# Rows gathered for the experts: transposed by TensorE instead of by DMA, and an expert's weight preparation moved into the next expert's first tile

## The chip, the core and the metric

The kernel runs on one core of a Trainium2 chip. The metric is the device time in microseconds (us) of one execution. Three runs of the kernel before took 850.43, 850.56 and 857.25 us; the median is 850.56.

## The reference: what is computed

Three layers follow each other. An attention over chunks of 64 positions (4 batches, 8 heads, 576 positions of 64) gives 2304 rows of 512 values. A mixture of 8 experts sends each row to the one expert with the largest gate value, and a plain two-matrix network with a hidden width of 2048 ends it (called FFN below).

```
x = attention(q, k, v)                       # 2304 rows of 512
probs = softmax(x @ w_gate); e = argmax      # one expert for each row
for each row i that expert e keeps:
    h = max(x[i] @ w1[e], 0)                 # 512 -> 1024
    out[i] = gate[i] * (h @ w2[e])           # 1024 -> 512
h = out @ w_in;  g = h * sigmoid(h);  result = g @ w_out      # FFN
```

## The kernel before, in words

Attention comes first and stores each row of x in the DRAM tensor `x_d`, as 512 high and 512 low halves in 16 bits and a factor. The experts follow, from 150.8 to 437.0 us of the profiled execution, then the FFN up to the end.

**A tile** (`moe_tile`, line 832) is up to 128 rows of one expert. Here the experts have 4, 1, 4, 3, 2, 1, 3 and 2 tiles, 20 in all, called t1 to t20 below (expert 0 has t1 to t4, expert 1 has t5, expert 2 t6 to t9, expert 3 t10 to t12, expert 4 t13 and t14, expert 5 t15, expert 6 t16 to t18, expert 7 t19 and t20). On TensorE (PE) a tile is 2 halves of 48 matmuls into `mh` (line 845), each value a sum of three products of high and low halves, and then 8 groups f = 0 to 7 of 3 matmuls into `myp` (line 866). Behind each half, ScalarE (ACT) writes `hh` (line 850) and VectorE (DVE) `hl` (line 851). The groups f = 0 to 3 read `hh` and `hl` of the first half, f = 4 to 7 those of the second. At the end the rows are scaled and scattered to `y_d` by a transfer that GpSimd (POOL) issues (line 882).

**A tile's rows** come by an indirect transfer on POOL (`gather`, line 819) into `xg`. The SyncE queue (SP) then issues a transfer that transposes them into `mxT` (`t_dma`, line 830, 128x8x128 values of 16 bits). SP runs its issues in the order of the program, and its transposes stand between the loads of weights (`w_piece`, lines 134 and 136) and of FFN weights (`f_load`, line 779).

**An expert's weights** (`w_prep`, lines 145 to 179) are two matrices, m = 0 (w1) and m = 1 (w2), of four 512 KB pieces each. Each piece is loaded, squared and summed on ACT (`sq`, line 157); the four sums are added over the partitions by a matmul with ones on PE (`red`, line 124, into the bank `fh`); DVE makes a scale of them (`sc`, lines 163 and 102 to 104); POOL writes the scaled high halves (`hi`, line 172) and DVE the low halves (`lo`, line 175). The buffer of a piece is loaded again once its low half is done (`lo_ld`, line 990).

**What sets the order.** The program is written out expert by expert. The first tile of an expert (j = 0) always runs; the code of the others stands in a branch on the count of rows (`more`, line 930), with an Else that does the rest of the preparation if the tile doesn't run. Work for the next expert is put into five places of the first tile (`slots`, 997 to 1004: 0 at its start, 1 behind the first half, 2 and 3 behind the second half, 4 at f = 6) and of the second and third tile (`arms`, 1035 to 1037). Before the change, `sq`, `red` and `sc` of the first matrix of the expert after next stand in the arms, `red` at f = 6 of the second tile or in the Else; `hi` of that matrix stands in slot 0 of the next expert's first tile, so it starts without a wait for a sum. The FFN weights are converted to 16 bits in the arms too (`f_conv`, lines 794 to 802), with the sums of squares of `w_in` on ACT (line 808).

The lines that the steps of the prediction touch: 819, 830, 845, 851, 866, 882 (tile), 124, 157, 163, 172, 175 (weights), 930 (branches), 439 and 444 (the transposes that the attention part already does on PE, with the copy out of PSUM on ACT).

Of the kernel before, what the change touches and what calls it, by code (L numbers as in the profile page):

```python
# [22 lines left out]
def attention_moe_ffn_kernel(  # L23
# [748 lines left out]

    def f_load(k):
# [54 lines left out]
    def t_dma(e, j):  # L828
        xg = xg_s[2 * (e % 2) + j % 2]
        nc.sync.dma_start_transpose(out=xT_s[slot(e, j)], in_=xg.bitcast(F16)[:, 0:2 * DM])  # L830

    def moe_tile(e, j, tok_i, c_i, keep, nxt, bg):
# [27 lines left out]
        for f in range(KF1):  # L860
            if f == 3 * KF1 // 4:
                bg(4)
                nxt(1)
# [29 lines left out]
    def t_next(e, j):  # L893
        t_dma(e, j)
        t_f1(e, j)
# [21 lines left out]
    t_dma(0, 1)  # L917
# [11 lines left out]
    def more(e, j, arms):  # L929
        with tc.If(n_e[e] > P * j) as cmp:  # L930
            def nxt(k):
                if k < 0 and j + 1 < NJ:
                    t_dma(e, j + 1)
                if k == 0 and j + 1 < NJ:
                    t_f1(e, j + 1)
                if k == 0 and j + 2 < NJ:
                    g_next(e, j + 2)
# [42 lines left out]
    m_dg = [st_s[1][3][:, (t + 1) * P:(t + 2) * P] for t in range(4)]  # L980
    for e in range(E):
# [4 lines left out]
        if not last:  # L986
            _, _, _, hi1, lo1 = prep[e + 1, 0]
# [9 lines left out]
            slots[0] = [lambda: g_next(e + 1, 0), *[lambda c=c: hi1(c) for c in range(4)]] if e else []  # L997
            slots[1] = [l1s[0], lambda: sq2(0), lambda: sq2(1)]
            slots[2] = [lambda: sq2(2), lambda: sq2(3), l1s[1], l1s[2], l1s[3]]
            slots[3] = [*([g2] if e else []), lambda: g_next(e + 1, 1)]  # L1000
            slots[4] = [red2, sc2, *[lambda c=c: hi2(c) for c in range(4)]]
        else:
            sp = [lambda c=c: f_split(0, c) for c in range(NSP)]
            slots = [[*cb, *cn], [], [], [], [lambda: f_red(0), lambda: f_sc(0), *sp]]

        def nxt0(k):
            if k < 0:
                if 0 < e < E - 1:
                    t_dma(e, 1)
            elif k == 0:  # L1010
                t_f1(e, 1)
                if last:
                    g_next(e, 2)
                else:
                    t_dma(e + 1, 0)
# [12 lines left out]
        if not last:  # L1028
            sqs, red, sc = [], [], []
            if e + 2 < E:  # L1030
                sq, r, c1, _, _ = prep[e + 2, 0]
                sqs, red, sc = [lambda c=c: sq(c) for c in range(4)], [r], [c1]
            arms[0] = [*l2s, *sqs, *red, *cb, *cn, *sc]
            arms[1] = [l2s[0:1], [l2s[1], *sqs[0:2]], [*l2s[2:4], *sqs[2:4], cb[0], cn[0]], [], [*red, *sc]]
            arms[2] = [[], cb[1:2], [*cb[2:], *cn[1:]], [], []]
        else:
            arms[0] = []
        more(e, 1, arms)
        if e + 2 == E:
            t_dma(E - 1, 1)  # L1040
# [214 lines left out]
```

## Time and profile before

| | |
|---|---|
| median of three runs | 850.56 us |
| the profiled execution: its time, and the span that the profile shows | 850.38 us, 848.6 us |
| PE busy | 722.5 us, 85% of the span |
| VectorE, POOL, ACT busy | 448.1, 359.4, 333.2 us |
| start of t1, of the FFN | 150.76, 437.02 us |

PE is the busiest engine, so the question for each piece of work is whether PE waits for it. A row of the timeline is a start, a duration, the engine, the line, the operation with the tile that it writes and those it reads, a count, and in brackets how long the engine was idle before it and what ended that. Consecutive equal instructions stand in one row.

### The profile page before, as it was taken

What the parts mean: (1) busy time and instruction counts of PE and PEld (TensorE: products, weight loads), DVE (VectorE), ACT (ScalarE), POOL (GpSimd) and SP (SyncE); (2) the same over time, 40 slices, a digit from 0 to 9 for tenths busy, and PEclk for the clock granted to TensorE, in tenths of its full rate; (3) what the DMA queues carried; (4) which work ended last, traced back from release to release, by engine and by line L of the source; (5) the groups of instructions that cost most, each with busy time, mean ns of one, the idle gap of its engine ahead of it and who ended that gap; (6) DMA issues with size and microseconds to landing.
All of it is one profiled execution on the core that took longest, in us unless ns stands there. A gap on an engine that the chain in (4) does not pass through costs nothing.

```text
span 848.6 us, 14692 instructions
## 1 busy us (share of the span) xinstructions
PE 722.5 (85%) x5526; PEld 440.5 (52%) x5526; DVE 448.1 (53%) x920; ACT 333.2 (39%) x615; POOL 359.4 (42%) x355
## 2 busy tenths in 40 slices
PE   4798764998489989569798776999999999999995
PEld 3677654765456756447553333444444444565442
DVE  4365886654794758678339999633322223222000
ACT  5586737443443536442134455322232223223010
POOL 3475632524571737665167535544223223212111
PEclk9797955899699999979899999999999999999999
DMA  7988983992986798895635235020001000001000
GB/s 170 230 231 206 191 239 59 306 273 56 303 246 162 177 235 239 241 237 123 135 72 102 73 125 124 1 51 1 1 37 38 1 1 37 14 1 39 13 37 38
DMA packets 133325, 103.20 MB, mean 122 GB/s; under 512 B 85472, under 2 KB 112096, under 8 KB 133216
## 3 DMA queue, kind: packets, MB, share of 16 engines
q1 hardware_dynamic: 126784, 83.41, 40.2%
q0 software_dynamic: 5760, 18.39, 7.3%
q8 instruction: 60, 0.98, 0.5%
q14 instruction: 49, 0.40, 0.2%
q10 hardware_dynamic: 672, 0.02, 0.0%
HBM read 73.45 MB, written 14.71 MB: 104 GB/s over the span
## 4 chain that ended last, share of the span: by engine, by line
PE 30%; DVE 8%; issue 7%; DMA 4%; POOL 2%; ACT 1%; POOLq 0%; ACTq 0%; DVEq 0%
PE ops L1143 14%; PE fh L1115 14%; DMA out_dram<-ob,yrow 3%; DVE g L1126 2%; DVE th L1121 2%; DVE wot L797 1%; DVE wot L802 1%; PE mh L845 1%; DVE wot L794 1%; DVE win L734 1%; DMA y_d<-yr,tabs 1%; PE myp L866 0%; POOL win L751 0%; POOL win L749 0%; POOL win L750 0%
## 5 line engine op out<-in xcount | busy, mean ns | idle before, releaser
L1143 PE MATMUL ops<-wot,gh 128*128 128x512 f16 x576 | 171.3, 379 | 0.0
L1115 PE MATMUL fh<-yT,win 128*128 128x512 f16 (+1 forms) x768 | 156.9, 355 | 7.0 <-DVE g L1126 7.0
L1130 POOL TENSOR_TENSOR gl<-g,gh 128x512 f16<-128x512 f32 (+1 forms) x80 | 91.9, 1151 | 163.8 <-ACT gh L1128 163.8
L1115 PEld LDWEIGHTS <-win 128*128 128x128 f16 x960 | 94.2, 98 | 118.1 <-issue 26.1
L845 PE MATMUL mh<-mxT,wsp 128*128 128x128 f16 x1920 | 125.6, 233 | 17.7 <-PEq L930 9.4
L845 PEld LDWEIGHTS <-wsp 128*128 128x128 f16 x1920 | 123.5, 106 | 24.1 <-issue 19.9
L1143 PE MATMUL ops<-wot,gl 128*128 128x512 f16 x288 | 109.2, 379 | 0.0
L1121 DVE TENSOR_TENSOR th<-fh,rb 128x512 f32<-128x512 f32 (+1 forms) x64 | 39.8, 622 | 130.7 <-PE fh L1115 130.7
L1122 ACT ACTIVATE th<-th,fi 128x512 f32<-128x512 f32 (+1 forms) x80 | 54.3, 679 | 133.8 <-DVE th L1121 132.9
L175 DVE SCALAR_TENSOR_TENSOR wsp<-st,s,wsp 128x1024 f16<-128x1024 f32 x64 | 99.6, 1591 | 6.0 <-POOL wsp L172 6.0
L866 PE MATMUL myp<-wsp,hh 128*128 128x512 f16 x320 | 96.5, 384 | 0.0
L1143 PEld LDWEIGHTS <-gh 128*128 128x128 f16 x576 | 56.4, 98 | 64.1
L172 POOL TENSOR_SCALAR wsp<-st,s 128x1024 f16<-128x1024 f32 x56 | 75.2, 1359 | 20.0 <-DVE inv L104 11.4
L1128 ACT CAST gh<-g 128x512 f16<-128x512 f32 (+1 forms) x80 | 45.9, 574 | 73.2 <-DVE g L1126 54.3
L157 ACT ACTIVATE junk<-st 128x1024 bf16<-128x1024 f32 x64 | 67.4, 1053 | 16.4 <-DMA st<-in_moe_w_dram 15.3
L1126 DVE TENSOR_TENSOR g<-fh,th 128x512 f32<-128x512 f32 (+1 forms) x80 | 50.7, 634 | 38.8 <-ACT th L1122 32.4
L866 PE MATMUL myp<-wsp,hl 128*128 128x512 f16 x160 | 61.6, 385 | 8.2 <-DVE hl L851 8.0
L819 POOL DMA_INDIRECT xg<-x_d,tabs x34 | 45.4, 1336 | 35.2 <-issue 9.5
L882 POOL DMA_INDIRECT y_d<-yr,tabs x20 | 23.5, 1175 | 79.3 <-DVE yr L879 36.8
L851 DVE SCALAR_TENSOR_TENSOR hl<-mh,hh 128x512 f16<-128x512 f32 x40 | 27.5, 687 | 48.3 <-ACT hh L850 48.3
L1115 PE MATMUL fh<-st,win 128*128 128x512 f16 x192 | 43.5, 379 | 10.6 <-DVE g L1126 9.3
L866 PEld LDWEIGHTS <-hh 128*128 128x128 f16 x320 | 30.7, 101 | 29.8 <-ACT hh L850 0.8
(194 smaller groups left out, 849.8 us busy)
## 6 DMA issues: line engine op xcount, KB each, us to landing
st<-in_moe_w_dram SPq DMA_DIRECT2D x64, 512.0 KB, 6.4
fs<-in_moe_w_in_dram SPq DMA_DIRECT2D x16, 512.0 KB, 7.0
fs<-in_moe_w_out_dram SPq DMA_DIRECT2D x16, 512.0 KB, 3.4
vbd<-in_v_dram SPq DMA_DIRECT2D x72, 64.0 KB, 3.4
x_d<-xr SPq DMA_DIRECT2D x9, 512.0 KB, 6.1
ku<-in_k_dram SPq DMA_DIRECT2D x6, 512.0 KB, 5.7
qu<-in_q_dram SPq DMA_DIRECT2D x6, 512.0 KB, 8.3
ku<-in_k_dram SPq DMA_DIRECT2D x2, 384.0 KB, 4.2
```

Of the source, the lines that this page charges most:

```text
L157: nc.scalar.activation(out=junk, in_=st[c], func=ACTF.Square, accum_out=n2[:, c:c + 1])
L172: hi_eng.tensor_scalar(sp[c][:, 0, :], st[c], s, 1.0, ALU.mult, ALU.mult)
L175: lo_eng.scalar_tensor_tensor(out=sp[c][:, 1, :], in0=st[c], scalar=s, in1=sp[c][:, 0, :], op0=ALU.mult, op1=ALU.subtract)
L845: nc.tensor.matmul(out=ps[:, f4, :], lhsT=a[c][:, part, f0:f0 + P], rhs=xt[:, rc, :], start=(n == 0), stop=(n == 3 * KD - 1),)
L866: nc.tensor.matmul(out=yp, lhsT=lh[:, f % 4, :], rhs=b[f // 2][:, part, (f % 2) * DM:(f % 2 + 1) * DM], start=(n == 0), stop=(n == 3 * KF1 ...
L1115: nc.tensor.matmul(out=hp[:, 0:n], lhsT=wv[:, part, c, :], rhs=yT_t[b](rc, n), start=(i == 0), stop=(i == 3 * KD - 1),)
L1121: nc.vector.tensor_tensor(out=th[:, 0:n], in0=hp[:, 0:n], in1=rb_t[b][:, 0:n], op=ALU.mult)
L1122: nc.scalar.activation(out=th[:, 0:n], in_=th[:, 0:n], func=ACTF.Sigmoid, scale=fi[:, 0:1])
L1126: nc.vector.tensor_tensor(out=g[:, 0:n], in0=hp[:, 0:n], in1=th[:, 0:n], op=ALU.mult)
L1128: nc.scalar.copy(out=gh[:, 0:n], in_=g[:, 0:n])
L1130: nc.gpsimd.tensor_tensor(out=gl[:, 0:n], in0=g[:, 0:n], in1=gh[:, 0:n], op=ALU.subtract)
L1143: nc.tensor.matmul(out=o_t[b][t], lhsT=lh[:, t * P:(t + 1) * P], rhs=wv[:, part, :], start=(f == 0 and i == 0), stop=(f == KFF - 1 and i = ...
```

## The change

The transposing transfer is removed. `x_tr` puts 8 PE transposes of 128x128 into one PSUM bank (the second of the two `fh` banks) and copies the bank to `mxT` on ACT. It is called behind the second half of each tile for the tile after it, and at f = 4 of an expert's first tile for the next expert's first tile. `red`, `sc` and `hi` of an expert's first matrix move to slot 1 of the expert before it, between the two halves of its first tile. The sums of squares of `w_in` (`cn`) move from the arms to slot 2 of the next expert.

```diff
--- before.py
+++ after.py
@@ -770,6 +770,8 @@
     ps_s = [mps.tile([P, 4, P], F32, name=f"mh{i}") for i in range(4)]
     yp_s = [mps.tile([P, DM], F32, name=f"myp{i}") for i in range(2)]
 
+    xtp = fh_s[1].bitcast(F16).rearrange("p (c t) -> p c t", c=2 * KD)
+
     def f_load(k):
         if k >= 2 * KFF:
             return
@@ -825,9 +827,11 @@
         f1 = f1_s[slot(e, j)]
         nc.vector.tensor_scalar(f1, xg[:, DM:DM + 1], w_fac[e, 0], w_fac[e, 1], ALU.mult, ALU.mult)
 
-    def t_dma(e, j):
-        xg = xg_s[2 * (e % 2) + j % 2]
-        nc.sync.dma_start_transpose(out=xT_s[slot(e, j)], in_=xg.bitcast(F16)[:, 0:2 * DM])
+    def x_tr(e, j):
+        xh = xg_s[2 * (e % 2) + j % 2].bitcast(F16)
+        for c in range(2 * KD):
+            nc.tensor.transpose(out=xtp[:, c, :], in_=xh[:, c * P:(c + 1) * P], identity=ident16)
+        nc.scalar.copy(out=xT_s[slot(e, j)], in_=xtp)
 
     def moe_tile(e, j, tok_i, c_i, keep, nxt, bg):
         xt, f1 = xT_s[slot(e, j)], f1_s[slot(e, j)]
@@ -858,6 +862,8 @@
         yp = yp_s[1 if j else 0]
         n = 0
         for f in range(KF1):
+            if f == KF1 // 2:
+                nxt(2)
             if f == 3 * KF1 // 4:
                 bg(4)
                 nxt(1)
@@ -891,7 +897,7 @@
         gather(e, j, tabs[:, 0, e, j:j + 1])
 
     def t_next(e, j):
-        t_dma(e, j)
+        x_tr(e, j)
         t_f1(e, j)
 
     def rest(e):
@@ -914,7 +920,6 @@
     t_next(0, 0)
     g_next(0, 1)
     g_next(1, 0)
-    t_dma(0, 1)
     w_load(1, 1)
     p10[1]()
     g_next(0, 2)
@@ -929,9 +934,8 @@
     def more(e, j, arms):
         with tc.If(n_e[e] > P * j) as cmp:
             def nxt(k):
-                if k < 0 and j + 1 < NJ:
-                    t_dma(e, j + 1)
                 if k == 0 and j + 1 < NJ:
+                    x_tr(e, j + 1)
                     t_f1(e, j + 1)
                 if k == 0 and j + 2 < NJ:
                     g_next(e, j + 2)
@@ -978,13 +982,14 @@
     NSP = 4
     conv_of = [[2 * e, 2 * e + 1] for e in range(E - 2)] + [[2 * E - 4, 2 * E - 3, 2 * E - 2], [2 * E - 1]]
     m_dg = [st_s[1][3][:, (t + 1) * P:(t + 2) * P] for t in range(4)]
+    cn_prev = []
     for e in range(E):
         last = e + 1 == E
         ops = [f_conv(c) for c in conv_of[e]]
         cb, cn = [lambda o=o: [f() for f in o[0:3]] for o in ops], [o[3] for o in ops]
         slots = [[], [], [], [], []]
         if not last:
-            _, _, _, hi1, lo1 = prep[e + 1, 0]
+            _, red1, sc1, hi1, lo1 = prep[e + 1, 0]
             sq2, red2, sc2, hi2, lo2 = prep[e + 1, 1]
 
             def lo_ld(m, c):
@@ -994,25 +999,27 @@
 
             l1s, l2s = [[lambda m=m, c=c: lo_ld(m, c) for c in range(4)] for m in range(2)]
             g2 = lambda: g_next(e, 2)
-            slots[0] = [lambda: g_next(e + 1, 0), *[lambda c=c: hi1(c) for c in range(4)]] if e else []
-            slots[1] = [l1s[0], lambda: sq2(0), lambda: sq2(1)]
-            slots[2] = [lambda: sq2(2), lambda: sq2(3), l1s[1], l1s[2], l1s[3]]
+            slots[0] = [lambda: g_next(e + 1, 0)] if e else []
+            slots[1] = [*([red1, sc1, *[lambda c=c: hi1(c) for c in range(4)]] if e else []),
+                        l1s[0], lambda: sq2(0), lambda: sq2(1)]
+            slots[2] = [lambda: sq2(2), lambda: sq2(3), *cn_prev, l1s[1], l1s[2], l1s[3]]
             slots[3] = [*([g2] if e else []), lambda: g_next(e + 1, 1)]
             slots[4] = [red2, sc2, *[lambda c=c: hi2(c) for c in range(4)]]
         else:
             sp = [lambda c=c: f_split(0, c) for c in range(NSP)]
-            slots = [[*cb, *cn], [], [], [], [lambda: f_red(0), lambda: f_sc(0), *sp]]
+            slots = [[*cb, *cn_prev, *cn], [], [], [], [lambda: f_red(0), lambda: f_sc(0), *sp]]
 
         def nxt0(k):
             if k < 0:
-                if 0 < e < E - 1:
-                    t_dma(e, 1)
-            elif k == 0:
+                return
+            if k == 0:
+                x_tr(e, 1)
                 t_f1(e, 1)
                 if last:
                     g_next(e, 2)
-                else:
-                    t_dma(e + 1, 0)
+            elif k == 2:
+                if not last:
+                    x_tr(e + 1, 0)
             elif not last:
                 t_f1(e + 1, 0)
             else:
@@ -1026,18 +1033,18 @@
 
         arms = {j: [[], [], [], [], []] for j in range(NJ)}
         if not last:
-            sqs, red, sc = [], [], []
+            sqs = []
             if e + 2 < E:
-                sq, r, c1, _, _ = prep[e + 2, 0]
-                sqs, red, sc = [lambda c=c: sq(c) for c in range(4)], [r], [c1]
-            arms[0] = [*l2s, *sqs, *red, *cb, *cn, *sc]
-            arms[1] = [l2s[0:1], [l2s[1], *sqs[0:2]], [*l2s[2:4], *sqs[2:4], cb[0], cn[0]], [], [*red, *sc]]
-            arms[2] = [[], cb[1:2], [*cb[2:], *cn[1:]], [], []]
+                sq = prep[e + 2, 0][0]
+                sqs = [lambda c=c: sq(c) for c in range(4)]
+            arms[0] = [*l2s, *sqs, *cb]
+            arms[1] = [l2s[0:1], [l2s[1], *sqs[0:2]], [*l2s[2:4], *sqs[2:4], cb[0]], [], []]
+            arms[2] = [[], cb[1:2], cb[2:], [], []]
         else:
             arms[0] = []
         more(e, 1, arms)
+        cn_prev = cn
         if e + 2 == E:
-            t_dma(E - 1, 1)
             with tc.If(n_e[E - 1] <= SPLIT0):
                 y0_load()
     with tc.If(n_e[E - 1] > SPLIT0):
```

Three places show how the instructions stand. The first is PE in the first tile of expert 1, at the step from f = 3 to f = 4 (`myp` is the tile's output, `hh_2153` and `hl_2155` belong to the first half, `hh_2154` to the second, `wsp` are the weights, `xg_2143` the gathered rows of expert 2's first tile). Before:

```order
L866 LDWEIGHTS hl_2155
L866 MATMUL myp_2172<-wsp,hl_2155 128x512
L866 LDWEIGHTS hh_2154
L866 MATMUL myp_2172<-wsp,hh_2154 128x512
L866 LDWEIGHTS hh_2154
```

Now, from the end of f = 3 (six more pairs of the same two rows of line 833 follow, and then the row of `hh_2154`):

```order
L872 LDWEIGHTS hl_2155
L872 MATMUL myp_2172<-wsp,hl_2155 128x512
L833 LDWEIGHTS xg_2143
L833 MATMUL fh_2136<-ident_85,xg_2143 128x128
L833 LDWEIGHTS xg_2143
```

Eight transposes now stand in PE's queue ahead of f = 4, and they wait for the gather of the next expert's rows.

The second is VectorE from the end of expert 0's last arm into the first tile of expert 1 (`st_66` to `st_69` are the pieces of expert 2's first matrix, `t`, `e`, `s`, `inv` the scale that `sc` makes). Before:

```order
L163 TENSOR_REDUCE t_2342<-fh_2135 128x1
L102 TENSOR_SCALAR e_2343<-t_2342 128x1
L103 TENSOR_SCALAR s<-e_2343 128x1
L104 TENSOR_SCALAR inv<-e_2343 128x1
L930 UNCONDITIONAL_BRANCH
L851 SCALAR_TENSOR_TENSOR hl_2155<-mh_2168,hh_2153 128x512
L175 SCALAR_TENSOR_TENSOR wsp<-st_66,s,wsp 128x1024
L851 SCALAR_TENSOR_TENSOR hl_2156<-mh_2169,hh_2154 128x512
L826 TENSOR_SCALAR yf_2152<-xg_2146,inv 128x1
```

Now:

```order
L935 UNCONDITIONAL_BRANCH
L855 SCALAR_TENSOR_TENSOR hl_2155<-mh_2168,hh_2153 128x512
L163 TENSOR_REDUCE t_2349<-fh_2135 128x1
L102 TENSOR_SCALAR e_2350<-t_2349 128x1
L103 TENSOR_SCALAR s<-e_2350 128x1
L104 TENSOR_SCALAR inv<-e_2350 128x1
L175 SCALAR_TENSOR_TENSOR wsp<-st_66,s,wsp 128x1024
L855 SCALAR_TENSOR_TENSOR hl_2156<-mh_2169,hh_2154 128x512
L828 TENSOR_SCALAR yf_2152<-xg_2146,inv 128x1
```

The scale, and with it the start of the high halves on POOL, now comes behind the first `hl` of the tile; the low half of the first piece still stands ahead of the second `hl`.

The third is SP at the start of expert 0's second tile. Before:

```order
L134 DMA st_66<-in_moe_w_dram 128x1024
L830 DMA_TRANSPOSE mxT_2148<-xg_2145 128x8x128
L134 DMA st_67<-in_moe_w_dram 128x1024
L134 DMA st_68<-in_moe_w_dram 128x1024
L134 DMA st_69<-in_moe_w_dram 128x1024
L930 COMPARE_AND_BRANCH
L830 DMA_TRANSPOSE mxT_2147<-xg_2143 128x8x128
L136 DMA st_70<-in_moe_w_dram 128x2x512
```

Now:

```order
L134 DMA st_66<-in_moe_w_dram 128x1024
L134 DMA st_67<-in_moe_w_dram 128x1024
L134 DMA st_68<-in_moe_w_dram 128x1024
L134 DMA st_69<-in_moe_w_dram 128x1024
L935 COMPARE_AND_BRANCH
L136 DMA st_70<-in_moe_w_dram 128x2x512
```

The transposes are gone from between the loads, here and in every other tile.

## Rows read from the trace of the kernel before

**Rows 1.** Stretches: length, busy us (PE, PEld, DVE, ACT, POOL), PE clock, DMA share, GB/s.

```profile
150.76:437.02 286.26, 235.38 (x2437) 172.49 (x2437) 182.54 (x355) 117.44 (x236) 150.02 (x118) 0.91 0.78 205
...
186.90:190.20 3.30, 3.30 (x37) 2.28 (x35) 0.50 (x4) 0.83 (x3) 0.00 (x0) 1.00 0.67 167
```

**Rows 2.** Waits of PE in the experts: in all, times, longest.

```profile
PE fh L124 <- ACT junk L157: 12.6, 4, 9.9
PE fh L124 <- DVE win L797: 11.6, 1, 11.6
PE mh L845 <- PEq L930: 9.4, 4, 4.5
PE myp L866 <- DVE hl L851: 8.0, 3, 3.0
```

**Rows 3.** Timeline of PE, expert 2: a tile without a wait.

```profile
253.17 5.52 PE L845 MATMUL mh<-mxT,wsp 128*128 128x128 f16 x96
...
258.53 0.59 PE L866 MATMUL myp<-wsp,hh 128*128 128x512 f16 x2
...
263.71 1.50 PE L845 MATMUL mh<-mxT,wsp 128*128 128x128 f16 x24
```

**Rows 4.** Timeline of PE, expert 0, end of t2 and start of t3.

```profile
174.98 0.39 PE L124 MATMUL fh<-n,ones 128*128 128x4 f32 x2 [1.74 <-ACT junk L157]
...
175.91 1.06 PE L866 MATMUL myp<-wsp,hh 128*128 128x512 f16 x2
...
177.19 6.50 PE L845 MATMUL mh<-mxT,wsp 128*128 128x128 f16 x96
```

**Rows 5.** Attention: transposes on PE (timeline), and their copy on ACT (line 444).

```profile
41.28 0.61 PE L439 MATMUL xtp<-ident,xr 128*128 128x128 f16 x8
41.83 1.09 PE L348 MATMUL sps<-kbd,qT 128*64 128x128 f32 x16
...
128.00 1.01 PE L439 MATMUL xtp<-ident,xr 128*128 128x128 f16 x8
...
L444 ACT COPY xt<-xtp x4: 992/1012/1013, 126.5 to 130.3; 128x1024 f16<-128x1024 f16 x4
```

**Rows 6.** Timeline of POOL, experts 1, 2 and 3.

```profile
205.36 4.40 POOL L172 TENSOR_SCALAR wsp<-st,s 128x1024 f16<-128x1024 f32 x4
...
222.36 1.86 POOL L882 DMA_INDIRECT y_d<-yr,tabs  x1 [0.17 <-issue]
...
231.55 0.99 POOL L819 DMA_INDIRECT xg<-x_d,tabs  x1 [7.33 <-PE mh L845]
...
280.62 4.40 POOL L172 TENSOR_SCALAR wsp<-st,s 128x1024 f16<-128x1024 f32 x4
```

**Rows 7.** Timeline of VectorE, first tiles of experts 1 and 3.

```profile
203.58 0.69 DVE L851 SCALAR_TENSOR_TENSOR hl<-mh,hh 128x512 f16<-128x512 f32 x1 [1.51 <-ACT hh L850]
...
281.65 0.69 DVE L851 SCALAR_TENSOR_TENSOR hl<-mh,hh 128x512 f16<-128x512 f32 x1 [4.57 <-ACT hh L850]
282.25 3.84 DVE L175 SCALAR_TENSOR_TENSOR wsp<-st,s,wsp 128x1024 f16<-128x1024 f32 x1
286.01 0.68 DVE L851 SCALAR_TENSOR_TENSOR hl<-mh,hh 128x512 f16<-128x512 f32 x1
```

**Rows 8.** Transfers in the experts, us to landing: transposes, then `y_d`, `xg` (min/median/max).

```profile
mxT<-xg SPq DMA_TRANSPOSE x26, 5.7
...
DMA to landing us min/median/max: 3.2/5.0/8.4
...
DMA to landing us min/median/max: 3.3/6.0/8.7
```

**Rows 9.** PE branches, line 930: after experts 0 and 6; ns min/median/max.

```profile
L930 PEldq COMPARE_BRANCH  x2: 197/1877/3557, 195.7 to 199.7; - x2
...
L930 PEldq COMPARE_BRANCH  x1: 7185/7185/7185, 401.2 to 401.2; - x1
```

## The prediction

> **What bounds the kernel now.** First the table of busy times over a stretch: between the first expert matmul (150.76 us) and the FFN's first (437.02) PE works 235.4 of 286.3 us, VectorE 182.5, POOL 150.0, ACT 117.4, and the DMA engines' share is 0.78 [rows 1]. So some 51 us of PE's idle time lie here, and the transfers are busier than any engine but PE. Then the list of PE's waits: 12.6 us in 4 times and 11.6 us once before a `red` matmul, 9.4 us in 4 times before a tile's first matmul behind a branch, 8.0 us in 3 times for `hl` [rows 2]. Last the timeline, to see which tiles are bound by PE. One without a wait runs from 253.17 to 263.71, 10.54 us at the full clock: 5.36 us for the two halves, then 8 groups of 0.648 us [rows 3]. There each instruction added to PE costs its whole time. The first tiles of the middle experts 1 to 6 are not of that kind: POOL and VectorE end last there, since the second `hl` stands behind a low half, which waits for POOL's high halves. In expert 3 POOL writes its four high halves in 280.62 to 285.02 [rows 6], the low half begins at 282.25 and ends only at 286.09, and `hl` follows at 286.01 (rows overlap by 0.08) [rows 7]. The change leaves attention alone, and the FFN only starts earlier or later, so the sum is made in the experts.
>
> **The sum, part by part**, against the profiled execution of 850.38 us, 0.18 below the median.
>
> A. *Start.* The first tile's transposition moves from a transfer to PE, into a time in which PE waits for that tile anyway. A transfer takes 5.7 us [rows 8], 8 transposes and a copy on ACT 0.55 + 1.0 [rows 5], but the transposes now stand ahead of PE's warm-up matmuls and these wait for the gather. I take +0.3, between 0 and +1.
>
> B. *Transposes on PE.* 8 of them took from 41.28 to 41.83, 0.55 us, at the full clock, and 1.01 in a stretch of lower clock [rows 5]. There are 28 groups. 15 stand where PE has no wait to hide them: two in t1, and one each in t2 to t4, t7 to t9, t11, t12, t14, t17 to t20 (t1's two count for t2 and t5). That is 15 x 0.55 = +8.25, up to +15 at the lower clock; the full clock is nearest, since the mean granted there is 0.91 [rows 1]. The other 13, twelve in the six middle first tiles (two each) and one at the start, are hidden by the waits of D and A. The copy on ACT, 1.0 us each [rows 5], lies on an engine with 169 us idle [rows 1]: nothing, unless it stands ahead of an `hh`, which it does not by its place behind the second half.
>
> C. *`red` leaves the second tiles.* In t2 PE waits 1.74 us for the sums, pays 0.28 for the matmul, and then has a lower clock: a group from 175.91 to 177.19, 1.28 for 0.65, and 6.50 for 5.52 in t3's halves [rows 3, 4]. 1.74 + 0.28 + 0.63 + 0.98 = 3.6. In t7 and t11 the waits are about half of the rest (12.6 less 9.9 and 1.7, 1.0 for both [rows 2, 4]) and 0.28 each; t14 only 0.28. Together -5.4; between -1.4 (the matmuls and no wait) and -7.
>
> D. *The high halves now wait for a scale inside the tile.* Before, POOL begins them when its queue is free: in expert 3 at 280.62, ahead of the first `hl` at 281.65 [rows 6, 7]. Now `red`, four small VectorE instructions and their signals stand between, behind that `hl`: 281.65 + 0.69 + 0.55 for the scale + 0.2 gives 283.1, 2.4 later; by the same two rows experts 4 and 5 lose 2.8 and 3.3. The second `hl`, 6.1 us behind the first high half (286.01 + 0.68 - 280.62), then comes later than PE wants it, by 1.3 us after PE has done the 1.1 us of the two transposes. In experts 1, 2 and 6 it costs nothing: POOL begins at 205.36 in expert 1 [rows 6], after the 205.0 that 203.58 + 0.69 + 0.55 + 0.2 gives [rows 7], because a gather stands ahead of it. So +8.5; between 0 (POOL and VectorE overlap better than they did) and +10 (all six lose a little).
>
> [...]
>
> E. *Less for the DMA engines.* A lone transposing transfer kept them 0.67 busy for 3.3 us, 2.2 us of all engines [rows 1]; 26 of these are 57 of 286 x 0.78 = 223, a quarter. Two kinds of waits that set the end should shrink. The scatter to `y_d` of a one-tile expert: at 222.36 POOL issues it, and the next gather follows at 231.55, because the branch's end waits for its landing [rows 6]; these landings run from 3.2 to 8.4, median 5.0 [rows 8]. And PE's far branch behind the third tile and its like: 3.56 us where the transfers are idle, 7.19 where they are busy [rows 9], of which PE waits up to 4.5 [rows 2]. With a quarter less traffic I take back a quarter to a third of the excess: 1.25 at each of two scatters, 1.0 at each of three branches (behind experts 3, 4 and 6), -5.5. Bounds: 0, and all to the idle values, 2 x 4.5 + 3 x 2.8, about -17.
>
> [...]
>
> F. *PE's waits of 11.6 and 9.9 us in the Else of one-tile experts* (1 and 5) vanish from the list, since `red` no longer stands there. They are worth 0: POOL's chain (second matrix's high halves, scatter from 222.36, landing, gather at 231.55, high halves of the next tile) ends later than PE's wait, and the next tile ends by it [rows 6]. PE then waits in the next tile instead. If it did not, the bound would be -21.5.
>
> G. *The sums of squares of `w_in`* move on ACT, from the arms to a place with 8 us of slack behind the second half: 0. SP's queue loses 26 issues that waited for gathers and stood ahead of weight loads; the loads mostly wait for VectorE's low halves, so 0, at most what E's bound already takes.
>
> Sum: 0.3 + 8.25 - 5.4 + 8.5 - 5.5 = +6.15. **Forecast 856.5 us**, its own range 851 to 861 (B and D a little smaller, E at its half or at 0).
>
> **Rivals.**
>
> *Relief is larger (about 850).* If E gives -12 rather than -5.5, because landings and branches of 5 to 8 us fall most of the way to 3.2 and 3.6, the time is 850. For it: a share of 0.78 with stretches near 1, and spreads of landings of more than 2 to 1 [rows 1, 8]. Against it: the 512 KB weight loads stay, and are the larger part.
>
> *Faster.* The relief of -12 together with D at 0, that is VectorE getting its turn between two high halves, gives 850.4 + 0.3 + 8.25 - 5.4 - 12 = 841.55, about 841. Against it stand the 3.84 us [rows 7]. [...]
>
> *Slower by more (862).* PE itself now waits for gathers: `x_tr` stands in PE's queue at f = 4 and behind the second half, and a gather that lands late stops every matmul behind it, where before only SP stood still. Gathers land in 3.3 to 8.7 us, median 6.0 [rows 8]. The gather for the next expert's first tile is issued at the start of the same first tile, about 7 us ahead of f = 4; that for the third tile about 9 us ahead. It decides from a landing of some 6 us (issue of 1 us included). Five or six places with 1 us each give +6, 862. For it: a third of the landings are that long. Against it: at f = 4 PE waits for `hl` anyway in four of six tiles, and with less traffic gathers land earlier.
>
> That the change doesn't do what it says is excluded: no transposing transfer of gathered rows is left on SP and the PE rows are there.
>
> **Chances.** Forecast 0.50, larger relief 0.22, faster 0.11, PE waiting for gathers 0.17. The 80% range leaves out most of the faster case and the far end of the slower one: 846 to 863. About 1% (8.5 us) is what a measurement can tell from no change. Faster by over 1% (below 842.1): the faster case's larger part and a tail, 0.11. Slower (above 859.1): the slower case and a sixth of the forecast's, 0.25. Within: 0.64.
>
> **What the changed profile would show.** For B: groups of 8 transposes of 0.55 us between second half and first group in tiles without a wait, so that such a tile takes 11.1 instead of 10.5. For C: no `red` in second tiles, t3 at 5.5. For D: in expert 3 the first high half about 2.2 us behind the end of the first half instead of about 0, a wait of PE for `hl` of 1 to 1.5 us in first tiles of experts 3, 4 and 5. For E: DMA share of the experts near 0.6, scatter landings behind experts 1 and 5 below 6.5, far branches of 4 to 6 us. For F: the waits for `red` gone, the waits for `hl` of experts 2 and 6 larger. The FFN would start near 443. Wrong would make it: hidden transposes that turn out not hidden (B near +15), waits of PE for `xg` of more than 3 us in all, or one-tile experts that end by PE and not by POOL (F).

## The result: 0.7% slower, and the profile after

The changed kernel takes 860.12 us, the kernel before 853.18 (medians of 16 runs each, taken side by side); the ratio is 1.0071, with a 95% interval of 1.005 to 1.0093, so about 6 us. The forecast was 6.15 us over the kernel before. Single executions of one kernel differ by some 8 us (850.4 to 858.4 before, 855.4 to 863.8 after). So totals are compared by medians below, and single traces only stage by stage. A ratio leaves out runs that lie more than 1.5% above the fastest of the same kernel; below these are two of about 857 us in one experiment and one each, of 1475.6 and 861.6 us, in two others.

The profiled execution after took 860.30 us, 9.92 more than that of before. The stretches, with the columns of [rows 1]:

```profile
0.00:145.18 145.18, 98.86 (x1206) 80.22 (x1206) 86.15 (x277) 88.83 (x164) 66.75 (x93) 0.85 0.80 190
145.18:156.03 10.85, 4.46 (x40) 4.21 (x39) 8.73 (x29) 5.28 (x5) 4.36 (x5) 0.50 0.64 200
156.03:445.49 289.46, 248.26 (x2654) 182.70 (x2653) 187.98 (x351) 142.93 (x263) 146.53 (x117) 0.92 0.56 174
445.49:858.50 413.01, 383.15 (x1854) 182.80 (x1854) 171.15 (x265) 122.89 (x212) 139.20 (x141) 0.98 0.13 38
```

Attention ends 3.20 us later than before (145.18 against 141.98), the start of the experts takes 2.07 more (10.85 against 8.78), the experts 3.20 more (289.46 against 286.26) and the FFN 1.4 more. The first of these is not the change: the instructions there are the same, and in the traces below this moment lies anywhere from 141.8 to 147.4 us, in kernels with and without either part of the change. The delay builds up over several waits for transfers and copies: by the gate's matmuls at 87.47 us (88.38 after), which waited 2.05 us for a transfer (4.74), it is 0.9 us, by those at 127.58 (130.74), which waited 2.82 us for a copy (4.56), it is 3.2.

What the change did lies in the 5.3 us of start and experts. The DMA share of the experts fell from 0.78 to 0.56. PE's busy time there rose by 12.9 us (248.3 against 235.4) and the stretch by 3.2, so most of the new work went into time in which PE had stood still. PE's waits in the experts after, to be held against [rows 2]:

```profile
PE mh L849 <- PEq L935: 14.8, 7, 3.2
PE fh L833 <- DMA xg<-x_d,tabs: 9.4, 3, 3.8
PE mh L849 <- issue: 7.2, 4, 2.4
PE myp L872 <- DVE hl L855: 6.3, 5, 1.8
```

The waits of 12.6 and 11.6 us for sums are gone but for 0.4. Those behind branches are more (two stand in one-tile experts, where a sum was waited for before), the longest fell from 4.5 to 3.2, and a new kind stands there: 9.4 us in 3 for gathered rows. By expert (time from first matmul to the next expert's): expert 0 45.3 against 49.3, experts 1 and 2 together 76.9 against 75.0, expert 3 41.4 against 40.1, expert 4 30.6 against 28.5, experts 5 and 6 66.7 against 65.8, expert 7 28.6 against 27.7.

A tile without a wait shows the price of 8 transposes on PE; from start to start it takes 10.99 us where it took 10.54 [rows 3], so 0.45 each:

```profile
178.62 5.52 PE L849 MATMUL mh<-mxT,wsp 128*128 128x128 f16 x96
183.98 0.61 PE L833 MATMUL fh<-ident,xg 128*128 128x128 f16 x8
189.61 5.52 PE L849 MATMUL mh<-mxT,wsp 128*128 128x128 f16 x96
```

And expert 3 shows the moved scale. POOL first (a start, a duration, and in brackets the idle time before), then VectorE, then PE in t11:

```profile
284.80 6.33 POOL L172 TENSOR_SCALAR wsp<-st,s 128x1024 f16<-128x1024 f32 x4 [1.13 <-DVE inv L104]
291.29 1.82 POOL L821 DMA_INDIRECT xg<-x_d,tabs  x1 [0.16 <-issue]
...
294.40 4.40 POOL L172 TENSOR_SCALAR wsp<-st,s 128x1024 f16<-128x1024 f32 x4
```

```profile
285.95 2.14 DVE L175 SCALAR_TENSOR_TENSOR wsp<-st,s,wsp 128x1024 f16<-128x1024 f32 x1 [1.35 <-POOL wsp L172]
288.01 0.68 DVE L855 SCALAR_TENSOR_TENSOR hl<-mh,hh 128x512 f16<-128x512 f32 x1
...
296.01 3.86 DVE L175 SCALAR_TENSOR_TENSOR wsp<-st,s,wsp 128x1024 f16<-128x1024 f32 x1
299.79 0.68 DVE L855 SCALAR_TENSOR_TENSOR hl<-mh,hh 128x512 f16<-128x512 f32 x1
```

```profile
298.04 0.62 PE L833 MATMUL fh<-ident,xg 128*128 128x128 f16 x8 [0.92 <-ACT junk L157]
...
300.53 0.39 PE L872 MATMUL myp<-wsp,hl 128*128 128x512 f16 x1 [1.44 <-DVE hl L855]
```

In the first tile the four high halves now take 6.33 us, not 4.40 [rows 6], and the low half beside them 2.14, not 3.84 [rows 7], so the second `hl` is in time and PE waits for nothing. But the high halves end at 291.13, 12.9 us after the tile began (10.0 before), and the gather whose rows t11 has to transpose comes behind them. The second matrix's high halves then stand straight behind a gather and take 4.40; the low half of 3.86 beside them stands ahead of t11's `hl`. So the bill comes one tile later: t10 is 0.7 us shorter than before, t11 2.0 longer.

### The profile page after: what moved, and what is told of

Same layout as the page of the kernel before. It is cut to its first block, busy times and chain, and to the rows that moved or that the text cites. A ratio compares the mean times of both kernels' runs of the same rounds, so it can differ in the third digit from the quotient of the medians.

```text
span 858.5 us, 15085 instructions
## 1 busy us (share of the span) xinstructions
PE 734.7 (86%) x5750; PEld 449.9 (52%) x5750; DVE 454.0 (53%) x920; ACT 359.9 (42%) x643; POOL 356.8 (42%) x355
## 4 chain that ended last, share of the span: by engine, by line
PE 30%; DVE 8%; issue 7%; DMA 3%; POOL 2%; ACT 1%; POOLq 0%; DVEq 0%; ACTq 0%
PE ops L1150 15%; PE fh L1122 14%; DMA out_dram<-ob,yrow 2%; DVE g L1133 2%; DVE th L1128 2%; DVE wot L799 1%; DVE wot L804 1%; DVE wot L796 1%; DVE win L734 1%; PE mh L849 1%; DMA y_d<-yr,tabs 1%; PE myp L872 0%; POOL win L751 0%; POOL gl L1137 0%; POOL win L749 0%
## 5 line engine op out<-in xcount | busy, mean ns | idle before, releaser
L849 PE MATMUL mh<-mxT,wsp 128*128 128x128 f16 x1920 | 123.1, 229 | 22.0 <-PEq L935 14.8
L849 PEld LDWEIGHTS <-wsp 128*128 128x128 f16 x1920 | 119.9, 104 | 29.8 <-issue 27.3
L175 DVE SCALAR_TENSOR_TENSOR wsp<-st,s,wsp 128x1024 f16<-128x1024 f32 x64 | 105.1, 1677 | 12.6 <-POOL wsp L172 12.6
L872 PE MATMUL myp<-wsp,hh 128*128 128x512 f16 x320 | 99.4, 393 | 0.0
L172 POOL TENSOR_SCALAR wsp<-st,s 128x1024 f16<-128x1024 f32 x56 | 72.2, 1304 | 21.3 <-DVE inv L104 9.8
L888 POOL DMA_INDIRECT y_d<-yr,tabs x20 | 26.3, 1314 | 86.5 <-DVE yr L885 38.3
L821 POOL DMA_INDIRECT xg<-x_d,tabs x34 | 43.5, 1278 | 35.6 <-issue 9.5
L854 ACT ACTIVATE hh<-mh 128x512 f16<-128x512 f32 x40 | 23.7, 594 | 58.6 <-PE mh L849 47.1
```

The costliest lines, as they stand in the source:

```text
L172: hi_eng.tensor_scalar(sp[c][:, 0, :], st[c], s, 1.0, ALU.mult, ALU.mult)
L175: lo_eng.scalar_tensor_tensor(out=sp[c][:, 1, :], in0=st[c], scalar=s, in1=sp[c][:, 0, :], op0=ALU.mult, op1=ALU.subtract)
L849: nc.tensor.matmul(out=ps[:, f4, :], lhsT=a[c][:, part, f0:f0 + P], rhs=xt[:, rc, :], start=(n == 0), stop=(n == 3 * KD - 1),)
L872: nc.tensor.matmul(out=yp, lhsT=lh[:, f % 4, :], rhs=b[f // 2][:, part, (f % 2) * DM:(f % 2 + 1) * DM], start=(n == 0), stop=(n == 3 * KF1 ...
```

## The experiments

All ratios are to the kernel before, timed in the same session. Two theories were set against each other first. Theory 1: the transposes on PE and their waits for gathers cost, and the moved sums give some back. Theory 2: the DMA engines' relief pays for the transposes, and the scale inside the tile costs.

**The transposes alone.** `red`, `sc`, `hi` and the norms back at their old places, `x_tr` kept:

```diff
-            slots[0] = [lambda: g_next(e + 1, 0)] if e else []
-            slots[1] = [*([red1, sc1, *[lambda c=c: hi1(c) for c in range(4)]] if e else []),
-                        l1s[0], lambda: sq2(0), lambda: sq2(1)]
+            slots[0] = [lambda: g_next(e + 1, 0), *[lambda c=c: hi1(c) for c in range(4)]] if e else []
+            slots[1] = [l1s[0], lambda: sq2(0), lambda: sq2(1)]
```

> The transposes move to PE; red, sc, hi and the norms stay where they were before. Theory 1 (the 28 groups of PE transposes and their waits for gathers are what costs, and the move of the sums gives some back): slower than the kernel before by 15 x 0.44 us in tiles without a wait, about 2 in first tiles, 4 at the two tiles that wait for a gather, less about 4 at the branches, so +8 to +10 us, ratio 1.010. Theory 2 (the relief of the DMA engines pays for the transposes, and the scale that now stands inside the tile is what costs): ratio 1.000, within 0.003.

1.005 (1.003 to 1.0071), medians 858.43 and 853.85. Between the theories: the transposes cost, but about half of what theory 1 said.

**The move alone**, transposes with the DMA engines (the same lines, the other way round, in the kernel before):

> The kernel before with red, sc, hi and the norms moved as in the change; the transposes stay with the DMA engines. Theory 1: faster than before by 4 to 5 us (no red in second tiles of experts 0, 2, 3, 4), ratio 0.995, and in expert 3's first tile the low half takes about 2.1 us, not 3.8. Theory 2: slower by about 6 us, ratio 1.007.

1.0062 (1.0032 to 1.0093). Theory 1 fell here, though what it said of expert 3 came true (the low half took 2.14 us). The waits:

```profile
PE myp L866 <- DVE hl L851: 19.7, 7, 5.1
PE mh L845 <- DMA mxT<-xg: 11.6, 5, 3.5
```

Each part alone costs half a per cent or more, both together 0.7%. So they seem not to add, but the two ratios multiplied are 1.011, and the 0.4% between that and 1.0071 is no larger than its own interval, also 0.4%. The trace has a reason why the move costs less beside the transposes on PE: with the move POOL's gathers come later, and a transposing transfer behind a late gather makes the tile wait (5 times, 11.6 us, 2.3 of them at the first tile). Transposes on PE and the copy are done 1.7 us after they can start (t11 of the changed kernel, 298.04 to 299.71).

**The next expert's transposes at the tile's end**, not at f = 4:

```diff
-            if f == KF1 // 2:
-                nxt(2)
...
             bounds_check=SKIP, oob_is_err=False,
         )
+        nxt(2)
```

> The changed kernel with the transposes for the next expert's first tile not at f = 4 but behind the tile's scatter, so PE waits for no gather in the middle of a tile. Theory 1: the waits for xg in t6 and t16 (3.6 and 3.9 us) go, and with them the low clock behind them; 3 to 4 us less than the changed kernel, ratio 1.003 to 1.004 to the kernel before. Theory 2, or if POOL's chain sets the end of these tiles anyway: as the changed kernel, 1.007.

1.0075 (1.0045 to 1.0106), as the changed kernel. The waits for `xg` at f = 4 went, and PE waited for `hl` there instead:

```profile
PE myp L870 <- DVE hl L855: 14.0, 5, 6.0
PE mh L849 <- PEq L934: 9.4, 4, 5.1
PE mh L849 <- ACT mxT L834: 6.7, 2, 4.5
```

In this trace experts 1 and 2 take 76.7 us and experts 5 and 6 67.5, in that of the changed kernel 76.9 and 66.7. So taking PE's stand for late gathers out of t6 and t16, 3.6 and 3.9 us, won nothing. Either it lies in front of a chain that ends later anyway, or the new waits for `mxT` at the start of t6 and t16, 2.2 and 4.5 us, ate what was won; this run does not part the two.

**Each group of transposes twice:**

```diff
-        for c in range(2 * KD):
+        for c in [*range(2 * KD), *range(2 * KD)]:
```

> The changed kernel with every group of 8 transposes done twice into the same bank. Theory 1 (15 groups with no wait to hide them, 0.44 each, and those of the first tiles of experts 3, 4 and 5 as well): 7 to 10 us over the changed kernel, ratio 1.015 to 1.019 to the kernel before. If the transposes are hidden in most tiles: within 2 us of the changed kernel, ratio 1.007 to 1.009.

1.0046 (1.0021 to 1.0072): not slower than the changed kernel, a miss for theory 1 and for its rival's number too. Tiles without a wait did take 11.43 us, 0.45 more again; but experts 1 and 2 took 73.9 us, not 76.9. There t5 began only after PE had waited 2.45 us for a branch of ACT (0.59 us for its own in the changed kernel), so the gather was done before the scale was ready; POOL stood idle before the high halves and took the other pattern (PE, POOL, then VectorE):

```profile
205.24 2.84 PE L849 MATMUL mh<-mxT,wsp 128*128 128x128 f16 x48 [2.45 <-ACTq L935]
```

```profile
210.11 6.33 POOL L172 TENSOR_SCALAR wsp<-st,s 128x1024 f16<-128x1024 f32 x4 [1.42 <-issue]
```

```profile
211.26 2.14 DVE L175 SCALAR_TENSOR_TENSOR wsp<-st,s,wsp 128x1024 f16<-128x1024 f32 x1 [1.25 <-POOL wsp L172]
213.32 0.68 DVE L855 SCALAR_TENSOR_TENSOR hl<-mh,hh 128x512 f16<-128x512 f32 x1
```

PE then waits in t5 for nothing (1.84 us for `hl` in the changed kernel), and the mean granted clock over t6 is 0.78 against 0.70 (windows of the doubled, then of the changed kernel):

```profile
220.10:243.25 23.15, 17.35 (x156) 14.18 (x157) 20.18 (x23) 13.82 (x25) 14.65 (x12) 0.78 0.77 243
```

```profile
218.11:244.16 26.05, 18.24 (x140) 12.93 (x141) 21.07 (x28) 13.76 (x25) 16.09 (x13) 0.70 0.71 238
```

That the experts lose nothing by 0.45 us more of PE's work in each group shows that the stages are coupled; which part of the gain is the clock and which the pattern is not settled by one trace.

**What sets the pattern.** In the kernel before, the gather of slot 0 behind the four high halves:

```diff
-            slots[0] = [lambda: g_next(e + 1, 0), *[lambda c=c: hi1(c) for c in range(4)]] if e else []
+            slots[0] = [*[lambda c=c: hi1(c) for c in range(4)], lambda: g_next(e + 1, 0)] if e else []
```

> The kernel before with the four high halves of slot 0 ahead of the gather of the next expert's rows instead of behind it. Theory A: what decides how POOL and VectorE share is whether the first high half follows straight on another POOL instruction (four take 4.40 us and the first low half 3.8 to 4.3) or starts POOL from idle (6.33 and 2.1). Then the four take 6.3 us here in first tiles, the low half about 2.1, PE's waits for hl fall from 8.0 to under 2 us, ratio to before 0.996 to 0.998. Theory B: it is decided by when the low half starts against the high halves; then 4.40 and about 4 stay, ratio 1.000.

0.9953 (0.9918 to 0.9987). That the time fell is not sure: the twelve runs spread from 843.2 to 857.1 us, and their median is 853.54 against 854.20 for the kernel before, which is 0.9992 with all runs taken in. For the pattern it is theory A: the high halves now start from idle in all six first tiles, and no low half beside them took over 2.2 us (t5 first, then t6, where the low half came when the high ones were nearly done):

```profile
208.84 6.33 POOL L172 TENSOR_SCALAR wsp<-st,s 128x1024 f16<-128x1024 f32 x4 [0.24 <-issue]
...
233.08 4.40 POOL L172 TENSOR_SCALAR wsp<-st,s 128x1024 f16<-128x1024 f32 x4 [6.93 <-DVE inv L104]
```

```profile
209.99 2.14 DVE L175 SCALAR_TENSOR_TENSOR wsp<-st,s,wsp 128x1024 f16<-128x1024 f32 x1 [0.48 <-POOL wsp L172]
...
236.85 1.70 DVE L175 SCALAR_TENSOR_TENSOR wsp<-st,s,wsp 128x1024 f16<-128x1024 f32 x1
```

In t5 the low half starts 1.15 us behind the first high half. In the kernel before it started 1.16 us behind it (the row below and 205.36 in [rows 6]) and took twice as long, so theory B is out:

```profile
206.52 4.31 DVE L175 SCALAR_TENSOR_TENSOR wsp<-st,s,wsp 128x1024 f16<-128x1024 f32 x1 [2.25 <-POOL wsp L172]
```

Two numbers of theory A were missed: the four took 6.33 us in t5 alone and 4.4 to 5.4 in the other five, where the low half came later or not at all beside them, and PE's waits for `hl` fell to 2.9 us, not under 2.

**The low half behind the second `hl`**, in the kernel before and in the changed one:

```diff
-            slots[1] = [l1s[0], lambda: sq2(0), lambda: sq2(1)]
-            slots[2] = [lambda: sq2(2), lambda: sq2(3), l1s[1], l1s[2], l1s[3]]
+            slots[1] = [lambda: sq2(0), lambda: sq2(1)]
+            slots[2] = [lambda: sq2(2), lambda: sq2(3), *l1s]
```

> The kernel before with the first low half of the next expert's first matrix behind the second hl of the first tile, not ahead of it. If the low half ahead of hl is what PE waits for in t5, t6 and t16: the waits for hl (8.0 us in 3) go, t6 and t16 end 2 to 3 us sooner, t5 does not since POOL's chain ends it; ratio 0.994 to 0.996. If POOL's chain sets the end of all three: ratio 1.000.

> The same edit in the changed kernel. If hl sets the end of t6 and t16: they end about 2 us sooner each, ratio to the kernel before 1.003. If the wait for the gathered rows at f = 4 (3.6 and 3.9 us) sets it instead: the wait for hl becomes a longer wait for xg, ratio 1.006 to 1.007 as the changed kernel.

0.9951 (0.9923 to 0.998) and 1.001 (0.9987 to 1.0032). So moving the low half behind `hl` won about 0.5% in both kernels. It doesn't explain the change: between these two 0.6% is left, nearly as between the original two (0.7%). Nor did the gain come where it was expected: in the kernel before, t6 is 3.0 us shorter and t7 4.6 longer, and the trace wins its time in experts 0 and 3 (2.3 and 3.1 us) and loses 2.8 in expert 4. In the changed kernel t6 and t16 end 0.6 and 1.5 us sooner, not 2.

**The scatter ahead of the second matrix's high halves**, in the changed kernel:

```diff
-            slots[4] = [red2, sc2, *[lambda c=c: hi2(c) for c in range(4)]]
+            slots[4] = [red2, sc2]
+            slots[5] = [lambda c=c: hi2(c) for c in range(4)]
...
             bounds_check=SKIP, oob_is_err=False,
         )
+        bg(5)
```

> The changed kernel with the tile's scatter to y_d issued ahead of the high halves of the second matrix (they now wait for the end of the tile). If POOL's chain of high halves, scatter, landing and next gather sets the end of experts 1 and 5: the landing is covered by the high halves, the gather there starts 3 to 5 us sooner, 6 to 8 us in all, ratio to the kernel before 0.998 to 1.000. If the later high halves hold up the low halves in the tiles behind as much: 1.006 or more.

1.0355 (1.0325 to 1.0384), the rival by far. The high halves come behind the tile's end, the low halves of the next tile stand ahead of its `hl`, and PE waits for those:

```profile
PE myp L872 <- DVE hl L855: 35.6, 10, 6.1
```

**All gathers ahead of the high halves**, with the low half behind `hl`; in the changed kernel, in the kernel with the move alone, and in the first of these with PE's 28 warm-up matmuls ahead of the first transposes:

```diff
-            slots[0] = [lambda: g_next(e + 1, 0)] if e else []
+            slots[0] = [lambda: g_next(e + 1, 0), g2, lambda: g_next(e + 1, 1)] if e else []
...
-            slots[3] = [*([g2] if e else []), lambda: g_next(e + 1, 1)]
+            slots[3] = [] if e else [lambda: g_next(e + 1, 1)]
```

> The changed kernel with the low half behind hl (as in the run before that did this) and, besides, the gathers for the expert's third tile and the next expert's second tile in slot 0, ahead of the high halves, not behind them. Theory: what the moved scale costs is that POOL's gathers come 3 to 4 us later and PE now stands for them in the tile behind; then the waits for xg in second tiles go (t6 and t16 keep theirs at f = 4), 2 to 3 us less than with the low half alone, ratio to the kernel before 0.997 to 0.999. Rival: the 28 transposes themselves and the start are what is left, ratio 1.001 as with the low half alone.

> The same two edits in the kernel with the move alone and the transposes left to the DMA engines. Theory: its waits for hl (19.7 us in 7) and for mxT (11.6 in 5) both come from POOL's later high halves, and go; the red of second tiles is gone too, and no transposes are added to PE: ratio to the kernel before 0.990 to 0.994. Rival: the transposing transfers stay late because SP and the DMA engines are full, ratio 1.000 or more.

> The first of these three with PE's 28 warm-up matmuls ahead of the first tile's transposes, not behind. If the start costs the changed kernel 2 us because the transposes hold the warm-up back behind the first gather: the first tile starts 2 to 3 us sooner after the end of the routing, 0 to 3 us in all (the first tile may run its first half at the lower clock), ratio 0.994 to 0.999. If the counts that PE reads set the start: no difference.

1.0137 (1.0094 to 1.0179), 1.0137 (1.01 to 1.0173) and 1.0119 (1.0083 to 1.0155). The theory that late gathers are the cost fell: they now come early, and the time rose by 1.3% over the run with the low half alone. In the second of the three the waits for `hl` fell from 19.7 to 6.8 us and those for `mxT` from 11.6 to 4.2, but 12.7 us for `hh` came in their place. In expert 1 the high halves begin 7.9 us after the tile, not 5.4 (timeline of POOL, first of the three; t5 begins at 202.7):

```profile
207.02 0.99 POOL L821 DMA_INDIRECT xg<-x_d,tabs  x1 [0.98 <-DVE t L163]
208.32 0.97 POOL L821 DMA_INDIRECT xg<-x_d,tabs  x1 [0.30 <-DMA y_d<-yr,tabs]
209.59 0.94 POOL L821 DMA_INDIRECT xg<-x_d,tabs  x1 [0.30 <-issue]
210.57 4.40 POOL L172 TENSOR_SCALAR wsp<-st,s 128x1024 f16<-128x1024 f32 x4
```

The experts took 300.7 us against 286.7 with the low half alone. Of these 14.0 us, 5.5 lie in experts 1 and 2 (79.5 against 74.0) and 7.9 in experts 5 and 6 (74.5 against 66.7); expert 3 is 1.6 longer, expert 4 1.1 shorter. So around the one-tile experts it fits that the time at which POOL has written the high halves sets the end, with all behind it: low halves, second scale, second high halves, scatter. This is argued, not shown, and as a rule for the middle experts it does not hold. In expert 3 the first high halves end 7.8 us after the tile's start with the transposes alone, 10.0 in the kernel before with the low half moved, 12.9 in the changed kernel and 8.3 in the next run, and the expert takes 37.4, 37.0, 41.4 and 43.6 us.

The warm-up's place moved the start as expected in the trace (8.3 us from the end of the routing to t1, not 10.9), but not the total by enough to tell.

**Both orders that had helped, together**, in the kernel before:

> The kernel before with both edits that helped alone: the gather of slot 0 behind the high halves, and the first low half behind the second hl. Theory (the time at which POOL ends an expert's first high halves sets the middle experts; three gathers ahead of them, 3.6 us in each of six first tiles, cost 14 us): the high halves start about 1.2 us sooner than with the low half's move alone, 3 to 5 us less, ratio to the kernel before 0.990 to 0.992. Rival: the two edits mend the same wait for hl, so together they give what each gave, ratio 0.995.

0.9991 (0.9959 to 1.0024), a miss for both. The second matrix's high halves now stand straight behind a gather in expert 3 (POOL), and PE waits in t11, for `hl` and then for `hh`; that tile takes 17.7 us, with 12.6 in the trace of the low half's move alone:

```profile
288.91 4.41 POOL L172 TENSOR_SCALAR wsp<-st,s 128x1024 f16<-128x1024 f32 x4
```

```profile
295.05 0.39 PE L866 MATMUL myp<-wsp,hl 128*128 128x512 f16 x1 [2.45 <-DVE hl L851]
...
299.44 0.60 PE L866 MATMUL myp<-wsp,hh 128*128 128x512 f16 x2 [2.06 <-ACT hh L850]
```

The run that moved the gather alone has this too: its second high halves in expert 3 stand straight behind a gather, and t11 takes 16.1 us. Expert 3 takes 42.9 us there and 43.6 here, where it took 40.1 in the kernel before and 37.0 with the low half's move alone. So the gather's move brings a wait of its own, which the trace of the low half's move does not have.

The fastest version found is the kernel before with the low half behind the second `hl`, some 0.5% below it.

## Why the prediction was right, and where it was not

The total was right (+6.15 forecast; medians +6.9, +6.1 by the ratio), in part by luck. As the trace gives the terms, A is about 0 (0.3 forecast), B +6.7 (8.25), C -6.4 (-5.4), D and F together +9.7 (8.5) and E -4.2 (-5.5): the sizes miss by up to 1.5 us, and the misses cancel. The mechanism was wrong in D, in E and in G, and in C it was half the reason.

A, *start*: 2.07 us, not 0.3. The warm-up matmuls stand behind the transposes, which wait for the gather, and PE reads the counts in between. But t1's halves then ran at a granted clock of 0.99, not 0.70 (5.56 us, not 7.70), so nearly all of it came back. With the warm-up ahead of the transposes the start took 8.3 us, not 10.9.

B, *transposes*: 0.45 us a group where a tile has no wait, not 0.55, and 15 of them, so 6.7 for 8.25. The doubled groups show that this price holds tile by tile but not as a sum.

C, *`red`*: t2 and t3 are 3.1 us shorter with two groups more, so about -4.0, forecast -3.6; t7 -0.85 with one group, so -1.3, forecast -0.75. In t11 nothing is left to see of it under D. But `red` is only half the reason. With the transposes alone `red` still stands in t2, and t2 and t3 are as short (11.12 and 10.99 us; 10.98 and 10.99 in the changed kernel, 13.58 and 11.52 before), because PE finds the sums ready. SP's loads of the four pieces are no longer parted by a transposing transfer, and ACT, which before waited for pieces 3 times, 2.9 us in all, waits for none (SP before, then SP and PE with the transposes alone):

```profile
160.23 3.17 SPq L830 DMA_TRANSPOSE mxT<-xg  x1
163.50 1.56 SPq L134 DMA_DIRECT2D st<-in_moe_w_dram  x3
```

```profile
159.79 5.61 SPq L134 DMA_DIRECT2D st<-in_moe_w_dram  x4
...
175.57 0.28 PE L124 MATMUL fh<-n,ones 128*128 128x4 f32 x2
```

With the move alone the pieces are late still (3.4 us of ACT's waits), but nobody waits for their sums there, and t2 and t3 take 11.55 and 11.18. So either part of the change takes this wait away, and together they take it away once.

D, *the scale inside the tile*: the size was near, the step failed in its mechanism. It said that PE would wait 1.3 us for `hl` in first tiles of experts 3 to 5. There is no such wait. The low half takes 2.14 us, not 3.84, beside high halves that now start from idle (1.13, 4.10 and 3.03 us of it) and not straight behind a gather, and these take 1.9 us longer. After their tiles' starts they begin 1.0, 4.2 and 3.5 us later in experts 3, 4 and 5 than before (2.4, 2.8 and 3.3 forecast; for expert 4 the prediction's own working, with `hl` at 320.34 and the high halves at 317.84, gives 3.9) and end 2.9, 6.2 and 5.4 us later, and that is paid in t11 and t14 (waits of 0.9 and 2.0 us at the transposes, 1.4 and 0.7 for `hl`). From t10 to t14 the time is 3.4 us longer; the shorter branches gave back 2.6 there, the missing `red` 1.1 (at the forecast's own price), and three groups cost 1.3, so D is about 5.8, forecast 5.2 for experts 3 and 4; the 3.3 for expert 5 can't be told from F. VectorE got its turn, as the rival *Faster* had it (in expert 3 the low half ended 3.0 us ahead of the last high half, not 1.1 behind it), and D cost its price all the same.

E, *less for the DMA engines*: the share fell as forecast (0.78 of 286 less 0.56 of 289 is 61 us, forecast 57), but the forecast's row was misread. The transfer of [rows 1] is not alone: in the first 1.1 of the 3.3 us a load of FFN weights ends. From 188.00 on the transposing transfer has the engines to itself and keeps them busy for 0.64 of 2.2 us, 1.4 us:

```profile
186.90:188.00 1.10, 1.10 (x7) 0.49 (x5) 0.00 (x0) 0.00 (x0) 0.00 (x0) 1.00 0.73 254
188.00:190.20 2.20, 2.20 (x32) 1.79 (x30) 0.50 (x4) 0.83 (x3) 0.00 (x0) 1.00 0.64 123
```

26 of these are 37 us. That 61 went, a few of them because three more weight loads were issued before the stretch began, is nearer to the forecast than its working deserved. And the landings did not follow: scatters 5.7 us in the median (5.0 before), gathers 6.1 (6.0) [rows 8]. The two scatters of one-tile experts landed after 7.4 and 7.2 us (7.7 and 6.7 before), so 0 there, forecast -2.5. The far branches did become shorter, 5.5 for 7.2 us behind expert 6 [rows 9]; PE waited 0.5, 2.2 and 1.6 us less behind experts 3, 4 and 6, -4.2, forecast -3.0:

```profile
L935 PEldq COMPARE_BRANCH  x2: 193/2862/5530, 410.3 to 416.2; - x2
```

That the relief did this is not shown. With the transposes alone, at nearly the same DMA share (0.57), the three waits are 1.9, 5.2 and 4.4 us, 1.8 less than before; with the move alone, at a share of 0.77, they are 3.4, 3.2 and 2.9, 3.8 less.

F, *the waits of 11.6 and 9.9 us*: right. They vanished and t5 and t6 together are 1.8 us longer, t15 and t16 2.1. POOL's chain ends there, from 223.65 (scatter) to 232.53 (gather), 8.9 us where it was 9.2 [rows 6]:

```profile
223.65 1.86 POOL L888 DMA_INDIRECT y_d<-yr,tabs  x1 [0.17 <-issue]
232.53 0.99 POOL L821 DMA_INDIRECT xg<-x_d,tabs  x1 [7.03 <-DMA fs<-in_moe_w_in_dram]
```

G: SP's lost issues were put at 0, and that step failed: they are what makes the sums of t2 ready in time (under C). The sums of squares of `w_in` were not moved alone in any run. In the changed kernel's trace no wait of PE is put down to them, with the low half moved as well 4.3 and 2.1 us are.

The rival of PE waiting for gathers came true as a wait, 9.4 us in 3, and not as a cost, as far as the run with the transposes at the tile's end shows. It leaves one trace: behind it t6 ends at a granted clock of 0.50, not 1.00, with 0.61 us for a matmul that took 0.39 before, and 4.48 us from the second `hl` to the end against 2.30 (the changed kernel, then the kernel before):

```profile
235.99 1.03 PE L833 MATMUL fh<-ident,xg 128*128 128x128 f16 x8 [3.58 <-DMA xg<-x_d,tabs]
...
239.68 0.61 PE L872 MATMUL myp<-wsp,hl 128*128 128x512 f16 x1 [1.81 <-DVE hl L855]
```

```profile
238.70 0.39 PE L866 MATMUL myp<-wsp,hl 128*128 128x512 f16 x1 [2.08 <-DVE hl L851]
```

Still open: what made the branches' waits shorter, how much of the doubled kernel's gain is the clock, and why the order of gather and high halves decides so much in t11.

## What to carry to other kernels

Look for the engine on which a stage ends; the waits of another engine in front of that end may be worth nothing. In the one-tile experts 21.5 us of PE's waits went and nothing was won, since POOL's chain from scatter to gather stayed at about 9 us. When a change has two parts, time each alone before pricing the sum, and look which wait each of them takes away: the late sums of t2 went with either part, so they could be won only once. And price a relief of a resource by what its waiting transfers show: here a quarter of the DMA engines' busy time went, and the median landings became no shorter (scatters 5.7 us for 5.0, gathers 6.1 for 6.0).

## What the hardware showed that was not expected

POOL's four high halves and VectorE's low half beside them mostly ran in one of two patterns: 4.40 us and about 4 when POOL came straight from the issue of a gather or scatter, 6.33 us and 2.14 when it started from idle. In the first, the low half ended 1.07 or 1.08 us behind the last high half in all six first tiles of the kernel before, whether it took 4.31 us or 2.36; in the second, in expert 3 of the changed kernel, it ended 3.0 us ahead of it. The prediction's rows had the first alone (4.40 and 3.84 us, [rows 6, 7]), and its sum kept to them.

Over the 14 traces, from expert 1 on, the four high halves stand 74 times straight behind such an issue with a low half starting beside them: 72 times they took 4.4 us, twice 6.34. From idle it was 6.3 to 6.4 in 66 of 86, 5.4 in 17, and 4.4 in the 3 where the low half started latest. So the start from idle is not the whole rule; what else selects is open. One of the two exceptions, in the changed kernel with the low half behind `hl` (POOL, then VectorE):

```profile
288.46 1.99 POOL L821 DMA_INDIRECT xg<-x_d,tabs  x1 [0.31 <-issue]
290.49 6.34 POOL L172 TENSOR_SCALAR wsp<-st,s 128x1024 f16<-128x1024 f32 x4
```

```profile
292.24 1.54 DVE L175 SCALAR_TENSOR_TENSOR wsp<-st,s,wsp 128x1024 f16<-128x1024 f32 x1
```

More work on PE (0.45 us in each of 28 places) did not make the experts longer in the trace, 285.3 us against 289.5.
